# An attention block's score bursts of ten: the first bank made in two halves

## The chip, the cores and the metric

The kernel runs on one core of a Trainium2 chip. The metric is device time in microseconds (us), from runs of the whole program. The engines that matter here are TensorE (PE in the profile, with its weight loads listed apart as PEld), ScalarE (ACT) and VectorE (DVE). PSUM, into which TensorE writes its products, has eight banks of 512 float32 columns on 128 partitions.

## The reference

Of the reference this is what matters. `x` is 2048 tokens of 1024 numbers; there are 32 heads of 32.

```python
qkv = (x @ wqkv).reshape(B, S, 3, H, Dh).transpose(2, 0, 3, 1, 4)
q, k, v = qkv[0], qkv[1], qkv[2]
scores = jnp.einsum("bhqd,bhkd->bhqk", q, k) * (Dh ** -0.5)
p = _softmax(scores, axis=-1)
a = jnp.einsum("bhqk,bhkd->bhqd", p, v).transpose(0, 2, 1, 3).reshape(B, S, D) @ wo
g = _sigmoid((x * gate_w).sum(-1, keepdims=True))
return g * a + (1 - g) * b        # b: a router over 64 experts, with one expert per head
```

The change touches the scores and their exponentials alone. The router, the projections and the last product with `wo` stand before and after that stage.

## The kernel before, in words

The kernel has three stages: projections and router (to about 627 us), attention (627 to 1616 us), and the output product. Everything is unrolled Python; each engine runs its instructions in the order in which the code issues them, and a framework adds the waits between engines, from the tiles that an instruction reads and writes.

**Scores.** For head `h`, the tile of keys `kt` (16 tiles of 128 keys) and the query block `qc` (4 blocks of 512 queries), one product on TensorE multiplies `K[:98, 128 keys]` (the stationary operand) with `Q[:98, 512 queries]` (the moving one) and fills one PSUM bank with 128 x 512 scores (line 1292). The 98 rows hold q and k in two parts each, and a shift of the exponent. ScalarE then writes the exponentials of the bank into the SBUF tile `P[h, kt]` (line 1301), a tile of 128 x 2048 numbers that `p_tile` hands out when its first block is due.

**The ring.** The banks come from `ring`, one PSUM tile of seven banks that is used round and round (`ring_banks`, `NB = 7`). An eighth bank is the output `O` of the product with the values. `on_ring` (lines 1247 to 1253) tells the framework about the ring: an instruction and an earlier one on another engine are declared independent when their sets of banks have none in common:

```python
if ins.ins.engine != other.ins.engine and not theirs & set(banks):
    tc.declare_no_dep(ins.ins, other.ins, reason="different banks of the ring")
```

**Order.** The stage goes in batches (lines 1523 to 1541). In each, `scores(s0, s1)` issues a burst of score products with their exponentials, then `pv` issues products of finished tiles of `P` with the values (line 1313, groups of four products side by side), then come the steps that are due (`todo`: loads, stores, sums) and the sums of `P` over key tiles on VectorE (`presum`, `add`, line 1353). A step is one bank. Heads 0 to 30 have 64 steps each, cut at 9, 18, 28, 37, 46, 55, 64, so that six bursts of a head have nine banks and the one from 18 to 28 has ten; the first batches of head 0 and the last ones of head 31 are cut otherwise.

**Cuts.** Within a burst, one exponential covers several neighbouring banks, up to the next cut (lines 1284 to 1287). Cuts lie at the end of a tile (four banks), where the ring wraps, at the burst's end, and, in a burst of more than seven banks, after each of the first `n - 7` banks. A burst of ten so begins with three exponentials of one bank each: its eighth, ninth and tenth products go into the banks of the first three. A burst of ten begins at step 18 of its head, in the third query block of key tile 4.

Of the kernel before, what the change touches and what calls it, by code (L numbers as in the profile page):

```python
# [13 lines left out]
AF = mybir.ActivationFunctionType  # L14
# [12 lines left out]
SCALE = 32 ** -0.5  # L27
# [5 lines left out]
def gated_mha_peer_kernel(ctx, tc, xT, wqkv, wv, wo, wq, k12, ug, v, out):  # L33
# [8 lines left out]
    nc = tc.nc  # L42
# [661 lines left out]
    for blk, (k, n) in enumerate(order):  # L704
        w, c = chunks[k]
# [442 lines left out]
    P, pools, keep, wk = {}, {}, None, None  # L1148


    def pairs_of(h):
        if h == H - 1:
            return (2, 4), (2, 6)
        if (h % 2 or (h % 4 and h < 17)) and h < 26 or h in (H - 4, H - 3):
            return (0, 2), (6, 8)
        return (0, 2), (3, 5), (6, 8)
# [5 lines left out]
    def p_tile(h, kt):  # L1162


        k = h * NT + kt
        n = [places for places, k0 in PLACES if k >= k0][-1]
        free = [i for i in range(n) if i not in (8, 9) or k < H * NT - 8]
        if k >= H * NT - 6:
            free = [i for i in free if i in ((0, 3, 7) if k >= H * NT - 2 else (1, 2, 3, 4, 5, 6))]
        i = min(free, key=lambda i: until[i])  # L1170
        pairs = pairs_of(h)
        until[i] = k + (18 if kt in [b for b, _ in pairs] else 10 if kt in [a for _, a in pairs] else 5)
        pool, name = ((pools["right"], f"P{i}") if i < 4 else (pools["left"], f"P{i}") if i < 8 else
                      (wk, f"P{i}") if i < 10 else (keep, ("vhl", "wo_raw2", "wo_raw3")[i - 10]))
        P[h, kt] = pool.tile([128, S], F32, name=name, bufs=1)
        return P[h, kt]
# [61 lines left out]
    ring = pss.tile([128, NB, 512], F32, name="ring")  # L1238
# [3 lines left out]
    def ring_banks(n):  # L1242
        i = [(ring_no[0] + k) % NB for k in range(n)]
        ring_no[0] += n
        return i

    def on_ring(ins, *banks):

        for other, theirs in users:
            if ins.ins.engine != other.ins.engine and not theirs & set(banks):  # L1250
                tc.declare_no_dep(ins.ins, other.ins, reason="different banks of the ring")
        users.append((ins, set(banks)))
        del users[:-6 * NB]
# [25 lines left out]
    def scores(s0, s1):  # L1279


        n = s1 - s0
        banks = ring_banks(n)
        cuts = {c for c in range(1, n + 1) if c == n or (s0 + c) % NQ == 0 or banks[c] == 0}
        cuts |= set(range(1, max(1, n - NB) + 1))
        if n <= 2 * NQ:
            cuts |= {c + 2 for c in range(NQ, n, NQ) if not cuts & {c + 1, c + 3}}
        c0 = 0
        for c, i in enumerate(banks):
            (h, kt), qc = divmod((s0 + c) // NQ, NT), (s0 + c) % NQ  # L1290
            K, Q = KQ[h % 2]
            on_ring(nc.tensor.matmul(ring[:, i, :], K[:98, kt * 128:(kt + 1) * 128],  # L1292
                                     Q[:98, qc * 512:(qc + 1) * 512], start=True, stop=True), i)
            if c + 1 not in cuts:
                continue
            m = c + 1 - c0
            q0 = qc + 1 - m
            if q0 == 0:
                p_tile(h, kt)
            i -= m - 1  # L1300
            on_ring(nc.scalar.activation(  # L1301
                P[h, kt][:, q0 * 512:(q0 + m) * 512].rearrange("p (a m) -> p a m", a=m),
                ring[:, i:i + m, :], AF.Exp, scale=SCALE), *range(i, i + m))
            c0 = c + 1
# [225 lines left out]
    for s1, v1 in batches:  # L1530
        if s1 > s0:
            scores(s0, s1)
        for part in parts_of(v0, v1):
            pv(*part)
        while NQ * (k + 1) <= s1:
            for f, a in todo.pop(k, []):
                f(*a)
            if k < NT * H:
                presum(*divmod(k, NT))
            k += 1  # L1540
        s0, v0 = s1, v1
# [292 lines left out]
```

## Time and profile before

| what | us |
|---|---|
| median of 3 runs | 1802.26 (1801.7 to 1802.41) |
| the profiled execution's own time | 1801.88 |
| its span, first to last instruction | 1800.1 |
| stage of attention in it | 627 to 1616 |
| granted TensorE clock | 1.00 of full speed |

Durations below come from the profiled execution, so sums are made against its own time. Lines of groups name the source line, the engine, the operation, the tiles written and read, the shape and the count; after the bar stand the busy time in us, the mean duration of one in ns, and the idle time of the engine just before them with what ended it. Lines of a timeline begin with the start and the duration in us; neighbouring instructions of one kind are merged, `x10` being their number, and a bracket gives idle time before them and its releaser. `ring<-Q,K` and `ring<-z,z` are the score products of odd and even heads. A PE record runs from its start to the writing of its result, so records of a stream overlap; a weight load's record runs beside the products.

### The profile page before, as it was taken

To read this page: it belongs to the slowest core of one execution; us is meant where nothing else is said; L and a number is where in the kernel's file an instruction comes from. 1 tells how busy PE (TensorE), PEld (TensorE's weight loads), DVE (VectorE), ACT (ScalarE), POOL (GpSimd) and SP (SyncE) were. 2 spreads that over 40 slices of the span, in tenths; PEclk is the share of its full clock that TensorE was granted. 3 is DMA by queue.
4 is the path that set the end of the run, shared out by engine and by line. 5 is a ranking of instruction groups with operands and counts; after the bars stand their busy time and mean duration, and the time that the engine had idled before them with its cause. 6 is when DMAs were issued, how large, how long until landed. Compare 5 with 4: busy or idle time off the path is not lost.

```text
span 1800.1 us, 27993 instructions
## 1 busy us (share of the span) xinstructions
PE 1793.7 (100%) x10559; PEld 1135.3 (63%) x10559; DVE 1502.7 (83%) x1685; ACT 1216.7 (68%) x1604; POOL 284.0 (16%) x353
## 2 busy tenths in 40 slices
PE   9999999999999999999999999999999999999999
PEld 7877777788888845555455554555554555547887
DVE  7868776358887779899899899999989989897774
ACT  4434321211333399999999999999999999993221
POOL 0222000026401201111111121121111121222000
PEclk9999999999999999999999999999999999999999
DMA  6788889823238688899899999898999999986761
GB/s 239 240 285 252 271 265 289 270 80 107 83 115 281 231 199 176 173 188 194 181 203 200 200 197 192 190 199 190 203 211 206 203 219 190 201 176 216 233 172 59
DMA packets 130454, 359.15 MB, mean 200 GB/s; under 512 B 18648, under 2 KB 56648, under 8 KB 104764
## 3 DMA queue, kind: packets, MB, share of 16 engines
q0 software_dynamic: 22352, 132.98, 36.3%
q1 hardware_dynamic: 87804, 188.42, 36.0%
q10 hardware_dynamic: 20160, 35.92, 7.0%
q8 instruction: 84, 1.38, 0.3%
q14 instruction: 54, 0.44, 0.1%
HBM read 173.72 MB, written 86.61 MB: 145 GB/s over the span
## 4 chain that ended last, share of the span: by engine, by line
PE 98%; DMA 1%; ACT 0%; SPq 0%; issue 0%; DVE 0%; ACTq 0%; DVEq 0%
PE ring L1292 28%; PE o L1313 26%; PE bk L155 13%; PE bk L711 10%; PE pa L155 6%; PE bk L758 5%; PE pa L1571 2%; PE bk L926 2%; PE bk L311 2%; PE bk L491 1%; PE pa L1578 1%; PE bk L395 1%; DMA wraw<-in_wqkv 1%; ACT P L1301 0%; SPq L82 0%; PE o L1326 0%
## 5 line engine op out<-in xcount | busy, mean ns | idle before, releaser
L1301 ACT ACTIVATE P<-ring 128x512 f32<-128x512 f32 (+3 forms) x986 | 808.1, 942 | 14.0 <-PE ring L1292 8.6
L1353 DVE TENSOR_TENSOR acc<-acc,P 128x1024 f32<-128x1024 f32 x408 | 469.7, 1219 | 22.1 <-ACT P L1301 22.1
L1313 PE MATMUL o<-P,V 128*32 128x512 f32 (+1 forms) x4040 | 412.6, 529 | 0.0
L1292 PE MATMUL ring<-Q,K 98*128 98x512 f32 x1024 | 268.7, 406 | 0.1
L1292 PE MATMUL ring<-z,z 98*128 98x512 f32 x1020 | 267.5, 406 | 0.1
L1292 PEld LDWEIGHTS ring<-Q,K 98*128 98x128 f32 x1024 | 182.6, 188 | 116.9 <-ACT P L1301 38.8
L1292 PEld LDWEIGHTS ring<-z,z 98*128 98x128 f32 x1020 | 182.1, 188 | 114.6 <-issue 37.8
L1313 PEld LDWEIGHTS o<-P,V 128*32 128x32 f32 x4040 | 111.5, 109 | 218.3 <-issue 198.6
L1353 DVE TENSOR_TENSOR rb<-rb,P 128x1024 f32<-128x1024 f32 x186 | 214.4, 1219 | 5.6 <-ACT P L1301 5.6
L1342 POOL DMA_DIRECT2D P<-P x60 | 55.7, 928 | 354.6 <-PE o L1313 141.1
L240 ACT ACTIVATE hi<-bk 128x512 fp32r<-128x512 f32 x40 | 23.7, 595 | 117.8 <-PE bk L711 98.7
L1301 ACT ACTIVATE wo_raw<-ring 128x512 f32<-128x512 f32 (+3 forms) x115 | 97.6, 942 | 0.6
L711 PE MATMUL bk<-xh,e 128*128 128x512 f32 x384 | 94.2, 394 | 0.0
L711 PE MATMUL bk<-xl,e 128*128 128x512 f32 x384 | 92.2, 389 | 0.0
L253 DVE TENSOR_TENSOR lo<-bk,hi 128x512 fp32r<-128x512 f32 x40 | 27.6, 690 | 68.8 <-ACT hi L240 66.5
L711 PEld LDWEIGHTS bk<-xh,e 128*128 128x128 f32 x384 | 71.0, 188 | 22.0 <-issue 3.4
L711 PEld LDWEIGHTS bk<-xl,e 128*128 128x128 f32 x384 | 72.1, 188 | 15.0
L101 DVE TENSOR_TENSOR e<-wraw,e 128x512 fp32r<-128x512 f32 (+3 forms) x64 | 55.1, 868 | 27.8 <-ACT e L100 27.3
L1301 ACT ACTIVATE vhl<-ring 128x512 f32<-128x512 f32 (+3 forms) x89 | 76.9, 940 | 0.9 <-PE ring L1292 0.2
L1353 DVE TENSOR_TENSOR acc<-acc,wo_raw 128x1024 f32<-128x1024 f32 x60 | 70.2, 1219 | 1.8 <-ACT wo_raw L1301 1.8
L100 ACT ACTIVATE e<-wraw 128x512 fp32r<-128x512 f32 (+3 forms) x64 | 44.6, 705 | 36.8 <-DMA wraw<-in_wqkv 16.2
L1361 POOL DMA_DIRECT2D acc<-acc x41 | 33.7, 822 | 221.0 <-DMA acc<-acc 83.3
(308 smaller groups left out, 2494.7 us busy)
## 6 DMA issues: line engine op xcount, KB each, us to landing
P<-P POOLq DMA_DIRECT2D x60, 1024.0 KB, 10.3
wqt<-in_wq SPq DMA_DIRECT2D x26, 1024.0 KB
wraw<-in_wqkv SPq DMA_DIRECT2D x30, 512.0 KB
acc<-acc POOLq DMA_DIRECT2D x21, 512.0 KB, 6.3
qdh<-hi ACTq DMA_DIRECT2D x32, 256.0 KB
qdl<-lo ACTq DMA_DIRECT2D x32, 256.0 KB
kdh<-hi ACTq DMA_DIRECT2D x32, 256.0 KB
kdl<-lo ACTq DMA_DIRECT2D x32, 256.0 KB
```

Of the source, the lines that this page charges most:

```text
L100: nc.scalar.activation(hi, src, AF.Copy)
L101: (on or nc.vector).tensor_tensor(out=lo, in0=src, in1=hi.bitcast(F32), op=OP.subtract)
L155: nc.tensor.matmul(ps, self.a[a][i][:, k, :], self.b[b][j][k], start=(not first and k == 0 and i == j == 0), stop=(k == HC - 1 and i == 1))
L311: nc.tensor.matmul(ps[32 * quad:32 * quad + 32, :], kpad[:, quad % 2, i, :], t[:, quad, :], start=(i == 0), stop=(i == 3))
L711: nc.tensor.matmul(ps, t[:, kc // HC, a, kc % HC], x_at(b, n, kc), start=first, stop=last)
L758: nc.tensor.matmul(ps, x_at(a, t // 4, kc)[:, tok], b, start=first, stop=last)
L926: nc.tensor.matmul(p, x_at(a, t // 4, kc)[:, tok], b, start=first, stop=last)
L1292: on_ring(nc.tensor.matmul(ring[:, i, :], K[:98, kt * 128:(kt + 1) * 128], Q[:98, qc * 512:(qc + 1) * 512], start=True, stop=True), i)
L1301: on_ring(nc.scalar.activation(P[h, kt][:, q0 * 512:(q0 + m) * 512].rearrange("p (a m) -> p a m", a=m), ring[:, i:i + m, :], AF.Exp, scale ...
L1313: nc.tensor.matmul(O[h][32 * qc:32 * qc + 32, c0:c1], Vt[g][:, kt, 32 * j:32 * j + 32], p[:, qc * 512 + c0:qc * 512 + c1], start=(kt == 0) ...
L1342: nc.gpsimd.dma_start(P[h, b], P[h, a], accum_op=OP.add)
L1353: nc.vector.tensor_add(out[:, c], a[:, c], b[:, c])
```

## The change

In a burst of more than nine banks, the first bank is made by two products of 256 columns each, into the left and the right half of the bank, and each half has an exponential of its own, issued right behind its product. The cut after that bank stays where it was; `c0 = 1` says that the next exponential begins at the second bank. All other bursts are as before. The halves are registered with `on_ring` under the same bank number `i`.

```diff
         for c, i in enumerate(banks):
             (h, kt), qc = divmod((s0 + c) // NQ, NT), (s0 + c) % NQ
             K, Q = KQ[h % 2]
-            on_ring(nc.tensor.matmul(ring[:, i, :], K[:98, kt * 128:(kt + 1) * 128],
-                                     Q[:98, qc * 512:(qc + 1) * 512], start=True, stop=True), i)
+            pieces = 2 if c == 0 and n > 9 else 1
+            for r in range(pieces):
+                w = 512 // pieces
+                cols = slice(qc * 512 + w * r, qc * 512 + w * r + w)
+                on_ring(nc.tensor.matmul(ring[:, i, w * r:w * r + w], K[:98, kt * 128:(kt + 1) * 128],
+                                         Q[:98, cols], start=True, stop=True), i)
+                if pieces == 2:
+                    if qc == 0 and r == 0:
+                        p_tile(h, kt)
+                    on_ring(nc.scalar.activation(P[h, kt][:, cols], ring[:, i, w * r:w * r + w],
+                                                 AF.Exp, scale=SCALE), i)
+            if pieces == 2:
+                c0 = 1
+                continue
             if c + 1 not in cuts:
                 continue
             m = c + 1 - c0
```

## The prediction, made before the result was known

> **What bounds the kernel now.** I began with the page's busy times and its chain of work that ended last, to see which engine and lines carry the end.
>
> ```profile
> span 1800.1 us, 27993 instructions
> PE 1793.7 (100%) x10559; PEld 1135.3 (63%) x10559; DVE 1502.7 (83%) x1685; ACT 1216.7 (68%) x1604; POOL 284.0 (16%) x353
> PE 98%; DMA 1%; ACT 0%; SPq 0%; issue 0%; DVE 0%; ACTq 0%; DVEq 0%
> ```
>
> The chain stands on PE, but a PE record lasts until its result is written, so "100% busy" doesn't exclude short stalls. The change touches only the attention stage, so I asked for the sums of that stretch (products of line 1292 run from 627 to 1616 us).
>
> ```profile
> core 0: us, PE busy (x) PEld busy (x) DVE busy (x) ACT busy (x) POOL busy (x), PEclk, DMA share, GB/s
> 627.00:1616.00 989.00, 988.89 (x6864) 498.42 (x6866) 920.43 (x823) 973.97 (x1223) 157.85 (x199) 1.00 0.92 195
> ```
>
> Here ScalarE is busy for 974 of 989 us too: two engines are nearly full, and the question is which one waits. The timeline of PE over one burst of ten and two of nine tells:
>
> ```profile
> 912.94 2.66 PE L1292 MATMUL ring<-Q,K 98*128 98x512 f32 x10
> 915.53 0.64 PE L1313 MATMUL o<-P,V 128*32 128x256 f32 x8
> 915.99 1.04 PE L1313 MATMUL o<-wo_raw,V 128*32 128x512 f32 x8
> 916.84 1.04 PE L1313 MATMUL o<-P,V 128*32 128x512 f32 x8
> 917.82 2.35 PE L1292 MATMUL ring<-Q,K 98*128 98x512 f32 x9
> 920.09 1.92 PE L1313 MATMUL o<-P,V 128*32 128x512 f32 x16
> 921.95 2.35 PE L1292 MATMUL ring<-Q,K 98*128 98x512 f32 x9
> 924.23 1.07 PE L1313 MATMUL o<-P,V 128*32 128x512 f32 x8
> ```
>
> Then the single instructions of the burst of ten, each from a narrow timeline: its first product; its first exponential, the first two together, and the third; the weight loads and the product at its end.
>
> ```profile
> 912.94 0.50 PE L1292 MATMUL ring<-Q,K 98*128 98x512 f32 x1
> 913.47 0.60 ACT L1301 ACTIVATE P<-ring 128x512 f32<-128x512 f32 x1 [0.21 <-PE ring L1292]
> 913.47 1.09 ACT L1301 ACTIVATE P<-ring 128x512 f32<-128x512 f32 x2 [0.21 <-PE ring L1292]
> 914.44 0.60 ACT L1301 ACTIVATE P<-ring 128x512 f32<-128x512 f32 x1
> 914.67 0.19 PEld L1292 LDWEIGHTS ring<-Q,K 98*128 98x128 f32 x1
> 915.10 0.19 PEld L1292 LDWEIGHTS ring<-Q,K 98*128 98x128 f32 x1 [0.24 <-ACT P L1301]
> 915.13 0.47 PE L1292 MATMUL ring<-Q,K 98*128 98x512 f32 x1
> ```
>
> Read it so. The first product ends at 912.94 + 0.50 = 913.44. A burst of nine takes 2.35 us, so its ends are (2.35 - 0.50) / 8 = 0.231 us apart, without a pause. Ten at that pace would end at 913.44 + 9 x 0.231 = 915.52; the last one ends at 915.13 + 0.47 = 915.60. So the burst of ten loses **0.08 us**, and the row of the waiting weight load says to whom: the tenth product goes into the third bank, whose exponential ends at 914.44 + 0.60 = 915.04. At the burst's start the other side waits: ScalarE stands idle for 0.21 us until the first bank is there. PE therefore sets the pace; ScalarE gets a short rest at a burst's start, and PE waits for it only at the tenth product. Anything that stops PE inside a burst moves every later burst.
>
> **The change part by part.** How often: bursts of ten are those from step 18 to 28 of heads 0 to 30 in the list of batches, 31 in all (head 31 has bursts of eight). In the timeline they are the PE rows with x10, of which these are the first and the last:
>
> ```profile
> 633.97 2.88 PE L1292 MATMUL ring<-z,z 98*128 98x512 f32 x10
> 1563.41 2.67 PE L1292 MATMUL ring<-z,z 98*128 98x512 f32 x10
> ```
>
> The prices of a half come from the groups by form:
>
> ```profile
> L1313 PE MATMUL o<-P,V 128*32 128x512 f32 x2760 | 336.7, 596 | 0.0
> L1313 PE MATMUL o<-P,V 128*32 128x256 f32 x1280 | 100.3, 385 | 0.0
> L1301 ACT ACTIVATE P<-ring 128x512 f32<-128x512 f32 x610 | 337.4, 631 | 13.9 <-PE ring L1292 8.6
> L1301 ACT ACTIVATE P<-ring 128x2048 f32<-128x2048 f32 x113 | 216.9, 1919 | 0.1
> L1599 ACT ACTIVATE z<-V 128x256 fp32r<-128x256 f32 x6 | 2.5, 412 | 4.8 <-DVE V L1598 4.7
> ```
>
> *Half a product.* 256 columns less shorten a product of line 1313 by 596 - 385 = 211 ns, but a row of 16 of those (four groups of four side by side) takes 1.92 us, (1.92 - 0.61) / 3 = 0.44 us per group with 0.61 us for one, where a score product takes 0.231 us. They stream at half the pace, so half a score product saves 211 / 2 = **0.106 us**.
>
> *Half an exponential.* From 512 to 2048 columns it grows by (1919 - 631) / 1536 = 0.839 ns a column, 0.215 us for 256. Starting on an idle ScalarE as here (0.60 us), a half takes 0.60 - 0.215 = **0.385 us**; L1599's 256 columns, another function, show 0.412 us. Two exponentials in a row start (1.09 - 0.60) = 0.49 us apart, halves so 0.49 - 0.215 = 0.275. So two halves cost ScalarE 0.55 instead of 0.49. The Trainium skill, page "ScalarE: Activation LUTs", section "What ACT_TABLE_LOAD costs", gives 186 ns and 0.833 ns a column for an ACTIVATE with immediate scale and bias: by it, as an estimate, 0.40 us for the half, and 31 x 0.015 = 0.5 us more in the sum below.
>
> *The wait that comes with it.* This decides. The second half's product writes into the bank that the first half's exponential reads. The framework adds waits by tiles, and the ring is one tile; `on_ring` takes them away only for pairs with no bank in common (line 1250). A planner that told columns apart would need no such declaration, as different banks are different columns. For the two halves nothing is declared, so I take it that the second product is held until the first half's exponential has ended. No row of before has a pair on two column ranges of one bank, so the cost is bounded: nothing (no wait) at one end, the full chain at the other. I take the full chain, since the nearest row, the load that waited 0.24 us for the exponential of its bank, is that wait.
>
> The Trainium skill, page "PSUM — Partial Sum Buffer", section "PSUM bank collisions raise a hardware error", asks to guard by bank and quadrant, not by address, since two engines on disjoint columns of one bank collide too. It speaks against this change and for the wait: by it the halves can't overlap. No run here shows a collision.
>
> *The chain, in the burst at 912.94.*
> 1. First half product ends 913.44 - 0.106 = 913.33.
> 2. Its exponential starts 0.03 later, as now (913.44 to 913.47): 913.36, and ends 913.36 + 0.385 = 913.75.
> 3. From an exponential's end to the end of a product of 512 columns that waited for it, the rows have 915.60 - 915.04 = 0.56 us. For 256 columns 0.56 - 0.106 = 0.45: the second half ends at **914.20**. In between PE has nothing to do: the products of the other nine banks, and the line 1313 groups behind them, stand behind the waiting instruction in program order.
> 4. Nine products follow at 0.231: the tenth bank ends at 914.20 + 2.08 = 916.28.
>
> Does its weight load, coming sooner after a short product, delay the second bank? The load at 914.67 belongs to the ninth product, which ends at 913.44 + 8 x 0.231 = 915.29, 0.62 later; the load at 915.10, with PE idle, is followed by its product's end after 0.50. So a load has 0.12 us in hand, just over the 0.106 that the half takes away. I take no delay; without that margin it costs 0.106 more.
>
> *What goes: the wait at the tenth bank.* The second half's exponential starts 914.20 + 0.03 = 914.23; the next 0.275 later, 914.51 (its product, 914.43, is there); the third at 914.51 + 0.49 = 915.00, ending 915.60. Then the tenth product could end at 915.60 + 0.56 = 916.16. It is due at 916.28, so that wait is gone: 0.08 us saved, and already in the sum. The eighth product, into the split bank, needs 914.23 + 0.385 + 0.56 = 915.18 and is due at 915.82: no wait.
>
> *Sum.* The burst's end moves from 915.60 to 916.28, **0.68 us**. ScalarE is 915.00 - 914.44 = 0.56 later, less than PE, so its rest before the next burst grows from about 0.2 by 0.1 and hides that. The bursts of nine have no pause in which PE could win back anything, and line 1313 reads tiles of earlier banks. 31 x 0.68 = **21.1 us**, on the profiled run's own 1801.88 us (span 1800.1 and 1.8 around it): 1823.0. The median of the runs is 1802.26, so 1823.3 beside it.
>
> **Rivals.**
>
> *A, the same wait at other prices.* The weight load late: 31 x (0.68 + 0.106) = 24.4 us, 1826.6. The half exponential at the full 0.60: 31 x (0.68 + 0.215) = 27.7, 1830.0. The second half's weights loaded while it waits: that spares at most the 0.12 by which a load runs ahead in the stream, 31 x 0.56 = 17.4, 1820. Against the last: the load at 915.10 itself waited.
>
> *B, no wait between the halves* (the other side: not slower). If columns are told apart, the second half's product ends at 913.33 + 0.106 + 0.02 = 913.46, exponentials start at 913.36, 913.63 and, for the second bank, 913.91 instead of 913.47 + 0.49 = 913.96; the tenth product, which is released by the third, comes 0.05 to 0.06 sooner. 31 x 0.06 = 1.9 us off: 1800.4. If the loads bind, PE needs 0.02 + 0.106 more, the tenth ends at 915.65, 0.05 later: 1803.8. It decides as soon as the first half's exponential no longer holds PE. For it: the waiting load shows only whole banks. Against it: the declaration by banks.
>
> *C, ScalarE sets the pace after all.* With 974 of 989 us busy, PE's lateness could be made up where PE waits for it. Then only ScalarE's delay counts, 0.56 less its rest of 0.21: 31 x 0.35 = 10.9, 1813. Against it: 2.35 us bursts of nine without a pause.
>
> *D, the wait spreads*: the second bank's product is held for the second half's exponential as well. It would end at 914.62 + 0.56 = 915.18 instead of 914.43: 31 x (0.68 + 0.75) = 44 us, 1846. Against it: different banks are declared independent.
>
> **How the numbers follow.** The forecast has 0.60, A 0.24, B 0.08, C 0.05, D 0.03. Predicted is the forecast's 1823.3. B, C and D, 0.16 together, are left out of the range, which holds the bounds of A and some of the way toward C: 1816 to 1830. A measurement of this kernel tells about 0.2% (3.6 us) from no change; B lies inside that in both of its forms, so same has 0.06, and 0.02 of its 0.08 go to faster, for a saving twice as large as worked out. Slower has the remaining 0.92.
>
> **What would show it.** In the changed kernel's trace a burst of ten begins with a product of 98x256, and the weight load of the second half has an idle time put down to the exponential of the first; the first half's exponential lasts about 0.39 us; the second half ends about 0.76 us after 913.44's counterpart; the load of the tenth product waits no more; from the first product's start to the last one's end it is about 3.3 us instead of 2.66; bursts of nine stay at 2.35, and ScalarE's rest before the burst that follows is longer. Wrong it would be if the second half follows the first within 0.25 us (B), or if bursts of nine become shorter or begin earlier than 0.68 us late (C).

## The result and the profile after

The changed kernel takes 1822.95 us (median; 1822.83 to 1824.05), the kernel before 1802.34 us (1801.7 to 1803.02): the ratio is 1.0116, with a 95% interval from 1.0098 to 1.0133. It is **slower by 20.6 us**, where 21 were forecast.

First the head and the chain of the page of the changed kernel, then its sums by stage (columns as before; the second row is the stage of attention).

```profile
span 1821.1 us, 28086 instructions
PE 1799.9 (99%) x10590; PEld 1140.4 (63%) x10590; DVE 1505.6 (83%) x1685; ACT 1222.4 (67%) x1635; POOL 284.2 (16%) x353
PE 80%; ACT 13%; issue 4%; DVE 2%; DMA 0%; SPq 0%; ACTq 0%; DVEq 0%
```

```profile
0.00:627.00 627.00, 624.72 (x2881) 493.89 (x2882) 457.62 (x684) 197.38 (x310) 111.75 (x131) 1.00 0.67 215
627.00:1637.00 1010.00, 994.87 (x6895) 502.22 (x6897) 922.51 (x823) 979.40 (x1254) 158.22 (x200) 1.00 0.91 191
1637.00:1821.10 184.10, 180.35 (x824) 144.27 (x812) 125.46 (x179) 45.65 (x72) 14.26 (x23) 1.00 0.60 169
```

The other two stages are as long as they were; attention took 989 us and takes 1010. PE has 31 more products and is busy 6 us longer there, but in 15 us of the stage it has nothing in flight, where there was 0.1 us before. And ScalarE, which had no part in the chain that ended last, now holds 13% of it. Where these come from is seen in one burst. This is PE's timeline over the burst that answers to the one at 912.94 (`wo_raw` and `vhl` in such rows are tiles of `P` too: `p_tile` puts some of them into places with these names):

```profile
919.03 0.38 PE L1296 MATMUL ring<-Q,K 98*128 98x256 f32 x1
919.89 2.45 PE L1296 MATMUL ring<-Q,K 98*128 98x256 f32 x10 [0.47 <-ACT P L1301]
922.27 0.64 PE L1325 MATMUL o<-P,V 128*32 128x256 f32 x8
922.73 1.04 PE L1325 MATMUL o<-wo_raw,V 128*32 128x512 f32 x8
923.58 1.04 PE L1325 MATMUL o<-P,V 128*32 128x512 f32 x8
```

These are ScalarE's rows, and the weight loads, of the same burst:

```profile
919.45 0.38 ACT L1301 ACTIVATE P<-ring 128x256 f32<-128x256 f32 x1
920.31 0.39 ACT L1301 ACTIVATE P<-ring 128x256 f32<-128x256 f32 x1 [0.47 <-PE ring L1296]
920.59 0.59 ACT L1313 ACTIVATE P<-ring 128x512 f32<-128x512 f32 x1
921.07 0.60 ACT L1313 ACTIVATE P<-ring 128x512 f32<-128x512 f32 x1
```

```profile
919.03 0.19 PEld L1296 LDWEIGHTS ring<-Q,K 98*128 98x128 f32 x1 [0.41 <-issue]
919.89 2.02 PEld L1296 LDWEIGHTS ring<-Q,K 98*128 98x128 f32 x10 [0.67 <-ACT P L1301]
```

And the chain in order of time (start, us, what), where "issue" is time between an end and the start of what it released:

```profile
919.10 0.33 PE ring L1296
919.43 0.02 issue
919.45 0.39 ACT P L1301
919.85 0.04 issue
919.89 2.45 PE ring L1296 x10
922.34 2.29 PE o L1325 x24
```

These rows show a relay. The first half's product ends at 919.41, its exponential runs from 919.45 to 919.83, and only at 919.89 does the second half's weight load begin. PE is empty for 0.47 us, and ScalarE then for 0.47 us in its turn. From there ten products run without a pause, and the last load waits for nobody. From the first product's start to the last one's end the burst takes 919.89 + 2.45 - 919.03 = **3.31 us**, where it was 2.66.

### The profile page after: what moved, and what is told of

Read it like the earlier page. It is cut to its first block, busy times and chain, and to the rows that moved or that the text cites. A ratio compares the mean times of both kernels' runs of the same rounds, so it can differ in the third digit from the quotient of the medians.

```text
span 1821.1 us, 28086 instructions
## 1 busy us (share of the span) xinstructions
PE 1799.9 (99%) x10590; PEld 1140.4 (63%) x10590; DVE 1505.6 (83%) x1685; ACT 1222.4 (67%) x1635; POOL 284.2 (16%) x353
## 4 chain that ended last, share of the span: by engine, by line
PE 80%; ACT 13%; issue 4%; DVE 2%; DMA 0%; SPq 0%; ACTq 0%; DVEq 0%
PE ring L1296 19%; PE o L1325 17%; PE bk L155 12%; ACT P L1313 10%; PE bk L711 10%; PE pa L155 6%; PE bk L758 5%; PE pa L1583 2%; PE bk L926 2%; DVE acc L1365 2%; PE bk L311 2%; PE bk L395 1%; PE bk L491 1%; ACT vhl L1313 1%; ACT wo_raw L1313 1%
## 5 line engine op out<-in xcount | busy, mean ns | idle before, releaser
L1313 ACT ACTIVATE P<-ring 128x512 f32<-128x512 f32 (+3 forms) x964 | 797.7, 950 | 14.7 <-PE ring L1296 13.2
L1296 PE MATMUL ring<-Q,K 98*128 98x512 f32 (+1 forms) x1039 | 271.5, 403 | 7.2 <-ACT wo_raw L1301 2.8
L1296 PE MATMUL ring<-z,z 98*128 98x512 f32 (+1 forms) x1036 | 270.6, 403 | 8.0 <-ACT P L1301 7.9
L711 PE MATMUL bk<-xh,e 128*128 128x512 f32 x384 | 94.2, 394 | 0.0
L155 PE MATMUL bk<-xh,e 128*128 128x512 f32 x288 | 68.5, 393 | 0.0
```

Source lines behind the costliest of these rows:

```text
L155: nc.tensor.matmul(ps, self.a[a][i][:, k, :], self.b[b][j][k], start=(not first and k == 0 and i == j == 0), stop=(k == HC - 1 and i == 1))
L711: nc.tensor.matmul(ps, t[:, kc // HC, a, kc % HC], x_at(b, n, kc), start=first, stop=last)
L1296: on_ring(nc.tensor.matmul(ring[:, i, w * r:w * r + w], K[:98, kt * 128:(kt + 1) * 128], Q[:98, cols], start=True, stop=True), i)
L1313: on_ring(nc.scalar.activation(P[h, kt][:, q0 * 512:(q0 + m) * 512].rearrange("p (a m) -> p a m", a=m), ring[:, i:i + m, :], AF.Exp, scale ...
```

## The experiments

Theory: **the hold**. The second half's product is held until the first half's exponential has ended, everything on PE stands behind it, and that is the whole loss. Rivals: the additional instructions are the loss (a product, its load, an exponential), or ScalarE's pace is. Except with the nines, the burst that answers to the one at 912.94 is compared throughout, by its time from the first product's start to the last one's end. The first four kernels are compared with runs of the kernel before that have a median of 1802.05 us, the others with runs of it that have 1802.06 us. The diffs are shortened: `...` stands for code left out, and the comments are this document's.

**Two products, one exponential.** The diff against before:

```diff
+            pieces = 2 if c == 0 and n > 9 else 1
+            for r in range(pieces):
+                w = 512 // pieces
+                cols = slice(qc * 512 + w * r, qc * 512 + w * r + w)
+                on_ring(nc.tensor.matmul(ring[:, i, w * r:w * r + w], K[:98, kt * 128:(kt + 1) * 128],
+                                         Q[:98, cols], start=True, stop=True), i)
```

> The first bank of a burst of ten is made by two products of 256 columns, but one exponential reads the whole bank, as before. Theory (the second half is held until the first half's exponential has ended, and that hold is the whole loss): no hold is left; the bank is ready about 0.02 us later (two streams of 0.106 + 0.02 for one of 0.231), the burst of ten takes about 2.68 us instead of 2.66, and the program 1802 to 1803 us. Rival (the additional product and its weight load are the loss): most of the 20.6 us stays, 1815 to 1823 us.

Measured: 1802.27 us, ratio 1.0 (0.9991 to 1.0009). The row of the eleven products, and the load at their end:

```profile
913.51 2.66 PE L1296 MATMUL ring<-Q,K 98*128 98x256 f32 x11
915.68 0.19 PEld L1296 LDWEIGHTS ring<-Q,K 98*128 98x128 f32 x1 [0.25 <-ACT P L1305]
```

The burst takes 2.66 us as before, and its last load waits for an exponential as before. Nothing is hidden behind that wait either: the second bank's product ends 0.74 us after the burst's start (913.85 + 0.40 - 913.51), where it was 0.73 before (913.27 + 0.40 - 912.94). A second product and a second weight load cost next to nothing: that rival is out.

**Both products first, then both exponentials.** Every instruction of the change, in another order:

```diff
+            for r in range(pieces):
+                on_ring(nc.tensor.matmul(...), i)      # half r of the bank
+            if pieces == 2:
+                for r in range(pieces):
+                    on_ring(nc.scalar.activation(...), i)
+                c0 = 1
+                continue
```

> Both halves of the bank are made first, then come their two exponentials: every instruction of the change is there, in another order. Theory: the second product waits for nothing, so the hold is gone. If the waits go by banks, the first exponential also waits for the second product: it starts about 0.03 us after that one's end, the two exponentials cost ScalarE about 0.06 more than one, and the tenth product moves by 0.08 in all: burst of ten about 2.74 us, program about 1804 to 1805 us. If waits went by columns, the first exponential would start at the first half's end and the burst would take about 2.60, the program 1800 to 1801. Rival (the additional instructions are the loss): about 1823 us.

Measured: 1804.64 us, ratio 1.0014 (1.0005 to 1.0023). PE's row, ScalarE's first exponential, and the load at the end:

```profile
914.01 2.73 PE L1296 MATMUL ring<-Q,K 98*128 98x256 f32 x11
914.55 0.39 ACT L1301 ACTIVATE P<-ring 128x256 f32<-128x256 f32 x1 [0.21 <-PE ring L1296]
916.24 0.19 PEld L1296 LDWEIGHTS ring<-Q,K 98*128 98x128 f32 x1 [0.30 <-ACT P L1312]
```

The burst takes 2.73 us: about 18 of the 20.6 us are gone though nothing was taken out. It shows the grain of the waits too. The first exponential starts 0.54 us after the first product, where in the changed kernel it started after 0.42: it waited for the second half's product as well, of which it reads nothing. That is what the Trainium skill, page "PSUM — Partial Sum Buffer", section "PSUM bank collisions raise a hardware error", asks for, a guard by bank and not by address. The rows show the guard that the framework sets; what the chip would do without it, no run here shows. Nor do they show whether the framework by itself goes by the bank or by the whole ring tile, since `on_ring` declares pairs on different banks independent in every kernel here.

**One product, two exponentials.**

```diff
             on_ring(nc.tensor.matmul(ring[:, i, :], ...), i)
+            if c == 0 and n > 9:
+                for r in range(2):
+                    on_ring(nc.scalar.activation(...), i)   # half r of the bank
+                c0 = 1
+                continue
```

> One product of 512 columns as before, and two exponentials of 256 columns for its bank. Theory: no hold; only ScalarE's price of a second exponential, which shows as the tenth product's wait: about 0.06 us a burst, burst of ten about 2.72, 31 x 0.06 = 1.9, program about 1804 us. Rival (ScalarE's additional instruction sets the loss through the whole stage): 10 us and more, 1813 or above.

Measured: 1804.27 us, ratio 1.0012 (1.0003 to 1.0021); PE's row, the two exponentials, and the load at the end:

```profile
913.64 2.73 PE L1292 MATMUL ring<-Q,K 98*128 98x512 f32 x10
914.17 0.66 ACT L1297 ACTIVATE P<-ring 128x256 f32<-128x256 f32 x2 [0.21 <-PE ring L1292]
915.86 0.19 PEld L1292 LDWEIGHTS ring<-Q,K 98*128 98x128 f32 x1 [0.30 <-ACT P L1308]
```

The burst takes 2.73, not 2.66: 31 x 0.07 = 2.2 us, what was measured. So ScalarE's second exponential has a price of its own, about a tenth of the loss, and it shows in the wait of the tenth product's load (0.30 us of idle time instead of 0.24). In the changed kernel the loads behind the hold run without such a wait, so the price isn't paid there.

**The halves in two banks.** The first bank's halves go to two neighbouring banks, so that they have none in common:

```diff
-        banks = ring_banks(n)
+        banks = ring_banks(n + (n > 9))
+        if n > 9:
+            pair, banks = banks[:2], banks[1:]
...
+            if c == 0 and n > 9:
+                for r, b in enumerate(pair):
+                    on_ring(nc.tensor.matmul(ring[:, b, :256], ...), b)
+                    on_ring(nc.scalar.activation(..., ring[:, b, :256], AF.Exp, scale=SCALE), b)
+                c0 = 1
+                continue
```

> The halves go into two neighbouring banks of the ring (the first 256 columns of each), so that they have no bank in common; a burst of ten uses eleven banks, and its last product waits for the third whole exponential, as before. Theory: the second half's product follows the first within 0.13 us, the first exponential starts about 0.1 us earlier than before, and the last product of the burst ends 0 to 0.06 us earlier than before: burst of ten 2.60 to 2.70 us (eleven products), program 1800 to 1803 us. Rival (the halves as such cost it, whatever their banks): about 1823 us. What stays unsure is the wrap of the ring, which falls elsewhere now and cuts other exponentials: up to 2 us either way.

Measured: 1800.63 us (1800.07 to 1801.71), ratio 0.9992 (0.9983 to 1.0002). PE's rows, and the two exponentials:

```profile
912.70 0.50 PE L1297 MATMUL ring<-Q,K 98*128 98x256 f32 x2
913.04 2.27 PE L1302 MATMUL ring<-Q,K 98*128 98x512 f32 x9
913.12 0.66 ACT L1299 ACTIVATE P<-ring 128x256 f32<-128x256 f32 x2
```

The instructions and their order in the burst's first bank are those of the change, but the halves have no bank in common; with it a burst takes eleven banks, and the ring wraps at other places. The second half follows at once, the first exponential starts 0.42 us after the first product instead of 0.53, and the burst takes 913.04 + 2.27 - 912.70 = 2.61 us instead of 2.66, 31 x 0.05 = 1.6 us. The median is 1.4 us below that of the kernel before, but the interval reaches over 1.0: it can't be told from no change by these runs. It is 22 us faster than the changed kernel.

**The hold covered.** The halves share the bank again, but the second half's product comes behind those of the next three banks:

```diff
+            if c == 0 and n > 9:
+                half(0)                   # product and exponential of the left half
+                c0 = 1
+                continue
...
+            if n > 9 and c == 2:
+                continue                  # its exponential is issued behind half(1)
+            if n > 9 and c == 3:
+                half(1)
```

> The halves share the bank, as in the change, but the second half's product comes behind the products of the second, third and fourth bank, and its exponential between those of the second and the third bank. Theory: the wait is still there (the second half may start only when the first half's exponential has ended), but PE has 0.69 us of other products ahead of it, so about 0.05 us of idle time is left of 0.47; burst of ten about 2.70 to 2.76 us, program 1803 to 1806 us. Rival (the split costs by its instructions, or ScalarE by its two exponentials): about 1823 us.

Measured: 1803.64 us, ratio 1.0009 (1.0 to 1.0018). PE's rows and the loads that waited:

```profile
913.33 0.38 PE L1295 MATMUL ring<-Q,K 98*128 98x256 f32 x1
913.56 0.86 PE L1302 MATMUL ring<-Q,K 98*128 98x512 f32 x3
914.25 0.33 PE L1295 MATMUL ring<-Q,K 98*128 98x256 f32 x1
914.42 1.62 PE L1302 MATMUL ring<-Q,K 98*128 98x512 f32 x6
914.19 0.19 PEld L1295 LDWEIGHTS ring<-Q,K 98*128 98x128 f32 x1 [0.21 <-ACT P L1297]
915.05 0.30 PEld L1302 LDWEIGHTS ring<-Q,K 98*128 98x128 f32 x2 [0.22 <-ACT P L1297]
```

The load of the second half still waits for the exponential, but three products run meanwhile, and its own product starts before the one ahead of it has been written. The burst takes 914.42 + 1.62 - 913.33 = 2.71 us, and about 19 of the 20.6 us are gone. So the wait alone isn't the loss; the loss is that PE had nothing else to do. The second load shows what is late next: the eighth product, into the split bank, now waits for the second half's exponential.

**Nines too.** The split in bursts of nine as well, with `n > 8` in place of `n > 9` in the changed kernel.

> The first bank of bursts of nine is split as well, 185 bursts beside the 31. Theory (PE's hold, each time in full, with nothing in the stage to win it back): a burst of ten gained 0.66 us, of which the wait at its tenth product gave back 0.08; a burst of nine has no such wait to lose, so each gains 0.74 us, from 2.35 to 3.09: 185 x 0.74 = 137, program about 1823 + 137 = 1960 us. Rival (ScalarE sets the pace, and only its own delay of 0.53 less its rest of about 0.1 counts): 216 x 0.4, about 1890 us.

Measured: 1967.79 us, ratio 1.092 (1.0903 to 1.0936), 8 us over the theory's 1960 and far from the rival's 1890: ScalarE's delay alone does not set the pace. A typical burst of nine, and one of the dear ones with ScalarE's rows (line 1390 is the copy of a head's output in `finish`):

```profile
1368.20 0.38 PE L1296 MATMUL ring<-z,z 98*128 98x256 f32 x1
1369.06 2.24 PE L1296 MATMUL ring<-z,z 98*128 98x256 f32 x9 [0.47 <-ACT vhl L1301]
```

```profile
702.43 0.39 PE L1296 MATMUL ring<-z,z 98*128 98x256 f32 x1
703.49 2.24 PE L1296 MATMUL ring<-z,z 98*128 98x256 f32 x9 [0.68 <-ACT P L1301]
702.57 0.60 ACT L1390 ACTIVATE osb<-o 128x512 f32<-128x512 f32 x1
703.06 0.38 ACT L1301 ACTIVATE P<-ring 128x256 f32<-128x256 f32 x1
```

The typical one takes 3.10 us instead of 2.35, 0.75 more; so a burst of ten, which grew by 0.65, did get back the 0.08 to 0.1 of its tenth product. The dear ones explain the 8 us: ScalarE is still at other work when the first half is there, the exponential starts late (703.06 instead of 702.86), and the hold grows by as much. Over the trace, 64 of the 185 bursts of nine start it late, 30 of them behind `finish`, about 9 us in all. The expectation had missed this.

**The hold alone.** One product and one exponential for the first bank, and behind them a product that makes the bank's right half once more; its result is read by nothing.

```diff
+            if c == 0 and n > 9:
+                on_ring(nc.scalar.activation(...), i)       # the whole bank
+                on_ring(nc.tensor.matmul(ring[:, i, 256:], ...), i)
+                c0 = 1
+                continue
```

> No split of the exponential: the first bank is made whole, its one exponential follows, and then the right half of the bank is computed once more by a product of 256 columns whose result nobody reads. It adds the hold alone, behind an exponential of 512 columns. Theory: that product ends 0.45 us after the exponential's end (914.07 + 0.45 = 914.52 in the burst at 912.94), the nine others follow, burst of ten 3.66 us instead of 2.66, 31 x 1.0: about 1833 us, more than the change, because the exponential is longer by 0.215 and its start later by 0.106. Rival (the loss is in the second exponential or the half widths): below 1810 us.

Measured: 1832.23 us, ratio 1.0166 (1.0151 to 1.0182). PE's rows and the exponential:

```profile
921.87 0.50 PE L1292 MATMUL ring<-Q,K 98*128 98x512 f32 x1
923.05 0.39 PE L1297 MATMUL ring<-Q,K 98*128 98x256 f32 x1 [0.69 <-ACT P L1295]
923.28 2.22 PE L1292 MATMUL ring<-Q,K 98*128 98x512 f32 x9
922.40 0.60 ACT L1295 ACTIVATE P<-ring 128x512 f32<-128x512 f32 x1 [0.21 <-PE ring L1292]
```

PE is empty for 0.69 us, and the product ends 923.44 - 923.00 = 0.44 after the exponential. The burst takes 923.28 + 2.22 - 921.87 = 3.63 us, 0.97 more than before, 31 x 0.97 = 30.1 us; measured were 30.2. About 0.11 us of the 0.97 is the additional product's own time (an estimate from the kernel with two banks, where the row of both halves lasts 0.50 us and the first half alone 0.39); the rest comes from the hold. So the hold makes the loss without a second exponential, and it grows with the exponential's length: PE is empty for 0.69 us behind an exponential of 0.60, and for 0.47 behind one of 0.38.

## Why the prediction was right, point by point

| step | predicted, us | measured in the burst at 919.03 |
|---|---|---|
| first half's product ends, after its start | 0.39 | 0.38 |
| its exponential takes | 0.385 | 0.38 |
| second half ends, after the first product's start | 1.26 | 919.89 + 0.38 - 919.03 = 1.24 |
| burst, from start to end | 3.34 | 3.31 |
| added to a burst | 0.68 | 0.65 |
| sum | 21.1 | 20.6 |

- **PE sets the pace.** Right: bursts of nine kept 2.35 us in the changed kernel's trace, and 31 x 0.65 = 20.2 us is nearly the whole difference of the medians. Between the traces of before and after, the burst behind a burst of ten starts later by 0.64 to 0.68 us each time (0.77 at the first one, of head 0, where ScalarE lags), 20.5 us over all 31; all other bursts together add 0.5. So nothing is won back on the way. ScalarE's rest before the burst that follows grew by the 0.1 that was forecast, though from 0.13 to 0.26 us (medians over the 31) and not from about 0.2. The rival by which ScalarE's delay alone counts (C) was tested with the nines and fell.
- **The second half waits for the first half's exponential.** This was the step that no row of before showed; it was argued from `on_ring`. Shown now by the row at 919.89, from the other side by the exponential that waits for both products, and by the two banks, where halves in the same order have no hold. The load of the second half is held as well, not its product alone, so the milder price in A (weights loaded during the wait) fell. The second bank's product is not held again, so D fell too.
- **The weight load hides.** Right: the nine products behind the second half end 2.45 - 0.38 = 2.07 us after it, 0.230 apart, and with two halves in a row eleven products take no longer than ten.
- **The wait at the tenth product goes.** Right: one row of ten loads from 919.89 on has no pause behind its first, and the nines, which had none to lose, grew by 0.1 more each.
- **Two exponentials cost ScalarE 0.06 more.** The burst with one product and two exponentials grew by 0.07; in the changed kernel this is hidden, as assumed. The page "ScalarE: Activation LUTs" of the Trainium skill, section "What ACT_TABLE_LOAD costs", gave by estimate 0.40 us for a half; the rows have 0.38 to 0.39, nearer to the slope of this kernel's own rows.
- **Sizes.** The hold's way came out 0.02 us too large and the nine products behind it 0.01, together 0.03 a burst or 0.9 us over 31. The first burst and the small slips elsewhere, which the sum had at nothing, gave about half of that back, so the closeness of 21.1 to 20.6 is in part luck.

The rival of the other side, no wait between the halves, was worked out at 1.9 us off. With the halves in two banks that is what the rows show (0.05 a burst, 1.6 us), so its price was about right and only its condition, no wait between halves of one bank, was not met. No kernel here keeps both halves in one bank and takes away only the declared wait; what the chip would do then stays open.

## What to carry to other kernels

Before splitting a tile so that its reader can start sooner, ask in which unit the waits are set: in this kernel a bank of PSUM is handed over as a whole, so two halves of one bank turn an overlap into a relay. The price is then not an instruction but a round trip (PE empty for 0.47 us: 0.38 of exponential and 0.09 for the handing over before and behind it), paid by everything that stands behind the waiting instruction in program order. Halves in two banks, or other work put ahead of the second half, take it away; so does the order alone, as the same two products and two exponentials take 1804.64 us when both products are issued first and 1822.95 us when the first exponential comes between them. And compare the prize first: it was at most 0.08 us a burst, the wait that the trace of before showed, against a hold that made the burst 0.65 us longer.

## What the runs showed that was not expected

The hold depends on what ScalarE is doing when the first half is ready: behind the 0.60 us copy of `finish` the same split held PE for 0.68 us instead of 0.47. And when the hold is covered, another wait comes up: the eighth product, for which the prediction had worked out no wait in the changed kernel, then waits for the second half's exponential.
